# One-hot rows of three token tiles by one comparison, in pooled attention followed by a top-1 mixture of experts

## The chip, the cores and the metric

The kernel runs on one core of a Trainium2 chip. The metric is the device time of one execution in microseconds. The core's engines are TensorE (PE in the profile, its weight loads PEld), VectorE (DVE), ScalarE (ACT), GpSimd (POOL) and SyncE (SP, which issues most DMAs). Each engine takes its instructions in the order in which the program wrote them and waits on semaphores for the others.

## What is computed

Inputs are q, k, v of 8 batches, 8 heads, 576 positions and 64 dimensions, a modality (0 or 1) for each of the 4608 tokens, and the weights of eight experts (512 to 1024 to 512).

```
k_p = k.reshape(B, H, 72, 8, D).mean(axis=3)          # v_p likewise
scores = scale * q @ k_p^T
attn = exp(scores - max) / (sum + 1e-9)
x = (attn @ v_p) as [4608, 512]
logits = x @ w_gate + modality_bias[modality_id]
e_idx = argmax(logits);  gate_w = softmax(logits)[e_idx]
out[token] = gate_w[token] * (relu(x[token] @ w1[e_idx]) @ w2[e_idx])
```

## The kernel before

**Two phases.** The attention comes first. It runs in 20 steps over the batches; a step works on one or two tiles of 128 tokens (36 tiles in all), in two halves of four heads: transposes of q, scores, the maximum (line 533), the subtraction (line 536), the exponential on ScalarE, transposes, and the product with v (lines 590 and 594), which VectorE scales into x and the logits (lines 610 to 616). GpSimd pools k and v of later batches meanwhile by adding halves (`fold`, lines 296 to 298) and multiplies out a remainder of v (line 361, the tile vw). The second phase is the mixture of experts: tokens are sorted by expert into slots of 256, gathered with an indirect DMA, and run through the expert's two matrices (lines 162 and 1143).

**Routing.** Between the phases each token needs a place. This is done in four groups of nine tiles (`route(g)`, lines 646 to 718): the logits are summed over the heads (664), biased (665) and compared with their maximum (666 to 675), gate weights are made (689 to 701), the rank of each token within its expert is a product on TensorE (`pe`, 677 to 688), and the rank is split into a column (`rh`) and a row in the column (`rkm`, then `rkf`, 711 to 715). Lines 716 and 717 make, for each of the nine tiles, the one-hot rows `arow[:, t, :]`: 128 numbers per token in bf16, of which the one at the token's row is 1. `iota_b` holds 0 to 127 in bf16 on every partition; `rkf` has one row number per partition and tile.

**Who uses the rows.** `arow` is the stationary operand of the products that turn ranks into tables of indices: line 776 in `early_table()` (lines 757 to 790), which takes the tiles of the first two groups and is followed by `finish_table` and four gathers (line 142); and line 1039 for the rest, in the second phase.

**What sets the order.** All engines' orders are written by hand. The steps of routing for the groups 0 to 2 aren't written at fixed places: `start(g)` (lines 820 to 826) puts them into a list, `drip`, and `gap(n)` (469 to 473) takes up to n of them off its head where VectorE's program has room: two between a maximum and its subtraction, one behind each of the small steps of `x_dve`, and two at the end of a half step. A step in `held` has TensorE instructions; it stops the list until `release()` writes it at a fixed place once per step of the attention. The list is first in, first out, so every entry that is taken up sooner or later moves all that stand behind it. The last group's steps are written in the second phase (`late`, lines 1091 to 1100): its one-hot rows come as `lr[21:]` in the first slot, with the column numbers behind them.

Of the kernel before, what the change touches and what calls it, by code (L numbers as in the profile page):

```python
# [11 lines left out]
BF16 = mybir.dt.bfloat16  # L12
# [3 lines left out]
ALU = mybir.AluOpType  # L16
# [6 lines left out]
P = 128  # L23
# [7 lines left out]
def kernel(  # L31
# [27 lines left out]
    NSLOT = (NTOK + EARLY_SLOTS * SLOT - 1 - E) // SLOT + E  # L59
    NCOL = 2 * NSLOT  # L60
    GT = 9
    GROUPS = [(GT * i, GT) for i in range(B // 2)]
    T_EARLY = GT * EARLY_GROUPS

# [12 lines left out]
    iota_b = cp.tile([P, P], BF16, name="iota_b")  # L77
# [12 lines left out]
    arow = cp.tile([P, NT, P], BF16, name="arow")  # L90
    oh = cp.tile([P, NT, E], BF16, name="oh")
    cum = cp.tile([P, len(GROUPS) + 1, E], BF16, name="cum")
    gate = cp.tile([P, NT], F32, name="gate")
# [89 lines left out]
    with ExitStack() as actx:  # L183
# [212 lines left out]
        def load_routing():  # L396
# [3 lines left out]
            for z in range(2):  # L400
                mz = mv.rearrange("(i z s) w -> z i s w", z=2, s=S)[z]
                nc.sync.dma_start(mod.rearrange("p (i t) w -> p i (t w)", t=GT)[:, :, 10 * z:10 * z + 8],
                                  mz[:, 0:512, :].rearrange("i (p j) w -> p i (j w)", j=4))
                nc.sync.dma_start(mod.rearrange("p (i t) w -> p i t w", t=GT)[64 * z:64 * z + 64, :, 4, :],
                                  mz[:, 512:S, :].rearrange("i p w -> p i w"))
# [55 lines left out]
        for n, (_, _, ts_) in enumerate(steps):  # L461
            for z, t in enumerate(ts_):
                tile_step[t] = (n, z)
        for g, (t0, n) in enumerate(GROUPS):
            for t in range(t0, t0 + n):
# [130 lines left out]
        def x_dve(t):  # L596
# [5 lines left out]
            if gi == 0:  # L602
                lgs[g] = late_p.tile([P, GT, H, E], F32, tag="lg", bufs=2, name=f"lg_{g}")
            xw = xbs[n if n < NX0 else NX0 + n % (len(xbs) - NX0)]
# [26 lines left out]
        def small(nm, g, shape, dt=F32):  # L631
            if g == len(GROUPS) - 1:
                return cp.tile(shape, dt, name=f"{nm}_{g}")
            return ap.tile(shape, dt, tag=nm, bufs=2, name=f"{nm}_{g}")

        def per_e(a, n):
            return a.rearrange("p (t o) -> p t o", o=1).to_broadcast([P, n, E])

        def per_t(a, n):
            return a.rearrange("p (o e) -> p o e", o=1).to_broadcast([P, n, E])  # L640

        def corner(n):

            return spare[0][:, 1, 4 * SPL + 12 * E:4 * SPL + 12 * E + n]

        def route(g):

            t0, n = GROUPS[g]
            sl = slice(t0, t0 + n)
            lg = small("lgr", g, [P, n, E])  # L650
            ex = small("ex", g, [P, n, E])
            m1 = small("m1", g, [P, n])
            m2 = small("m2", g, [P, n])
            sm = small("sm", g, [P, n])
            dc = small("dc", g, [P, E])
            rs = small("rs", g, [P, n, E])
            rk = small("rk", g, [P, n])
            rki = small("rki", g, [P, n], I32)
            rkm = small("rkm", g, [P, n], I32)
            rkf = small("rkf", g, [P, n])  # L660
            V = nc.vector
            ops = []
            add = ops.append
            add(lambda: V.reduce_sum(lg, lgs[g].rearrange("p t h e -> p t e h"), axis=AX.X))
            add(lambda: V.tensor_add(lg, lg, bias_all[:, sl, :]))
            add(lambda: V.reduce_max(m1, lg, axis=AX.X))

            def sub():
                V.tensor_tensor(lg, lg, per_e(m1, n), op=ALU.subtract)
                nc.scalar.activation(ex, lg, AF.Exp)  # L670
            add(sub)

            add(lambda: V.scalar_tensor_tensor(lg, lg, 0.0, per_t(w8, n), op0=ALU.is_equal, op1=ALU.mult))
            add(lambda: V.reduce_max(m2, lg, axis=AX.X))
            add(lambda: V.tensor_tensor(oh[:, sl, :], per_t(w8, n), per_e(m2, n), op=ALU.is_equal))

            def pe():
                if g == len(GROUPS) - 1:
                    pr = ps_tr.tile([P, n, E], F32, tag="tr", name=f"pr_{g}")
                else:  # L680
                    pr = corner(n * E).rearrange("p (t e) -> p t e", e=E)
                nc.tensor.matmul(pr, tri, oh[:, sl, :], start=True, stop=False)
                nc.tensor.matmul(pr, ones, cum[:, g:g + 1, :].to_broadcast([P, n, E]), start=False, stop=False)
                for i in range(n - 1):
                    m = n - 1 - i
                    nc.tensor.matmul(pr[:, i + 1:n, :], ones, oh[:, t0 + i:t0 + i + 1, :].to_broadcast([P, m, E]),
                                     start=False, stop=(i == n - 2))
                rts[g] = pr
            add(lambda: V.reduce_sum(sm, ex, axis=AX.X))
            add(lambda: V.tensor_scalar_add(sm, sm, 1e-9))  # L690
            add(lambda: V.reduce_sum(dc, oh[:, sl, :].rearrange("p t e -> p e t"), axis=AX.X))

            def gates():
                V.reciprocal(gate[:, sl], sm)
                for z in range(2):
                    b = 2 * g + z
                    nc.sync.dma_start(xs[b * S:b * S + 512, D:D + 1].rearrange("(p j) o -> p (j o)", j=4),
                                      gate[:, t0 + 5 * z:t0 + 5 * z + 4], allow_slow_non_contiguous=True)
                    nc.sync.dma_start(xs[b * S + 512:(b + 1) * S, D:D + 1],
                                      gate[64 * z:64 * z + 64, t0 + 4:t0 + 5], allow_slow_non_contiguous=True)  # L700
            add(gates)
            add(lambda: V.tensor_add(cum[:, g + 1, :], cum[:, g, :], dc))
            held.add(pe)
            add(pe)
            if g >= EARLY_GROUPS:
                add(lambda: V.tensor_tensor(rs, rts[g], per_t(adjv, n), op=ALU.add))  # L706
                add(lambda: V.tensor_mul(rs, rs, oh[:, sl, :]))
            else:
                add(lambda: V.tensor_tensor(rs, rts[g], oh[:, sl, :], op=ALU.mult))
            add(lambda: V.reduce_sum(rk, rs, axis=AX.X))  # L710
            add(lambda: V.tensor_copy(rki, rk))
            add(lambda: V.tensor_single_scalar(rkm, rki, 127, op=ALU.bitwise_and))
            add(lambda: V.tensor_single_scalar(rki, rki, 7, op=ALU.logical_shift_right))
            add(lambda: V.tensor_copy(rkf, rkm))
            add(lambda: V.tensor_copy(rh[:, sl], rki))
            for i in range(n):
                add(lambda i=i: V.tensor_scalar(arow[:, t0 + i, :], iota_b, rkf[:, i:i + 1], None, op0=ALU.is_equal))  # L717
            return ops

        def first_expert():  # L720
# [76 lines left out]
        def at(hook, n, *fns):  # L797
            hook.setdefault(n, []).extend(fns)

        for n, (b, jj, _) in enumerate(steps):  # L800
            if b + 1 < B:
                if jj == 0:
                    m = n if b else n + 1
# [3 lines left out]
                if jj == 1:  # L807
                    m = n if b else n + 1
# [8 lines left out]

        for g in range(len(GROUPS) - 1):
            n = s1_of[2 * g + 1] + 2
            def start(g=g):  # L820
                ops = route(g)
                m = GROUPS[g][1]
                drip.extend(ops[:-m])
                if g == 0:
                    drip.extend(first_expert())
                drip.extend(ops[-m:])
            at(hook_0, n, start)
            if g == EARLY_GROUPS - 1:
                at(hook_0, n, lambda: drip.extend(early_table()))
# [137 lines left out]
        while drip:  # L967
            release()
            gap()
        loads(N + 1)  # L970
        last_route = route(len(GROUPS) - 1)
        for fn in last_route[:7]:
            fn()
# [7 lines left out]
    op = [[ps_op.tile([P, 512], F32, name=f"op{i}_{z}") for z in range(2)] for i in range(2)]  # L981
# [12 lines left out]
    V = nc.vector  # L994
# [106 lines left out]
    t = table(c4 + 6, NCOL, 4)  # L1101
# [189 lines left out]
```

## Time and profile before

| | us |
|---|---|
| three executions | 641.79, 639.85, 642.85 (median 641.79) |
| the profiled execution | 639.47 |
| its span, from the first to the last instruction | 637.8 |
| busy: PE, DVE, ACT, POOL | 601.1, 433.8, 343.8, 198.9 |
| granted TensorE clock, mean over the span | 0.990 |

Busy shares are means over both phases. The attention takes about the first 190 us, and the engines share its work; the mixture of experts takes the rest, and TensorE is busy nearly without a pause in it. For one instruction, its duration says how long it took with its wait for a shared resource, if there was one; how long it holds up its queue is the distance from its start to the start of the next, which can be less, since an instruction of VectorE begins a little before the one ahead has ended.

### The profile page before, as it was taken

How to read it: one execution, taken by the hardware profiler on the slowest of the kernel's cores; microseconds unless marked ns; L12 is line 12 of the kernel's file. 1: busy time of each engine (PE TensorE's matmuls, PEld its weight loads, DVE VectorE, ACT ScalarE, POOL GpSimd, SP SyncE). 2: the span in 40 equal slices, each digit the busy share in tenths (PEclk: the TensorE clock that was granted, in tenths of full speed). 3: DMA queues.
4: the chain of work that ended last, by engine and by line, in shares of the span. 5: the costliest groups of instructions: out<-in, count | busy, mean ns of one | idle time of the engine just before them, and what ended most of it. 6: DMA issues, size and time to landing. Idle time of an engine off the chain costs nothing.

```text
span 637.8 us, 12547 instructions
## 1 busy us (share of the span) xinstructions
PE 601.1 (94%) x4223; PEld 544.8 (85%) x4223; DVE 433.8 (68%) x940; ACT 343.8 (54%) x640; POOL 198.9 (31%) x277
## 2 busy tenths in 40 slices
PE   4799898989899999999999999999999999999992
PEld 3699797888798999999999999999999999999881
DVE  4778989999977578666566566656656566656541
ACT  2667566677441455555555555555556555555530
POOL 6689967563000221320320221231131231131230
PEclk9899999999999999999999999999999999999997
DMA  9999979764201901201210461220225410120120
GB/s 255 290 300 337 350 208 362 223 202 143 67 35 51 315 33 36 68 34 35 68 41 28 148 201 51 67 65 8 63 75 180 145 55 17 52 68 18 51 75 17
DMA packets 63406, 77.18 MB, mean 121 GB/s; under 512 B 15455, under 2 KB 42079, under 8 KB 63328
## 3 DMA queue, kind: packets, MB, share of 16 engines
q1 hardware_dynamic: 57168, 55.98, 28.4%
q0 software_dynamic: 6160, 20.26, 9.7%
q8 instruction: 38, 0.62, 0.4%
q14 instruction: 40, 0.33, 0.2%
HBM read 119.94 MB, written 19.45 MB: 219 GB/s over the span
## 4 chain that ended last, share of the span: by engine, by line
PE 76%; DVE 13%; DMA 7%; issue 1%; ACT 1%; SPq 0%; DVEq 0%; ACTq 0%
PE op L1143 30%; PE hp L162 30%; DMA out_dram<-ob,sidx 6%; PE av L590 3%; PE sc L526 3%; PE xt L153 2%; DVE mx L533 2%; DVE sb L536 2%; PE av L594 2%; DVE xb L614 2%; PE pq L501 1%; PE ph L162 1%; PE pp L555 1%; DVE arow L717 1%; DMA k<-in_k_dram 1%
## 5 line engine op out<-in xcount | busy, mean ns | idle before, releaser
L135 ACT CAST hl<-raw 128x1024 fp32r<-128x1024 f32 x138 | 144.8, 1049 | 138.6 <-PE op L1143 136.6
L162 PE MATMUL hp<-xh,hl 128*128 128x256 f32 x1152 | 186.2, 284 | 0.6 <-issue 0.6
L162 PEld LDWEIGHTS hp<-xh,hl 128*128 128x128 f32 x1152 | 166.0, 189 | 11.5 <-issue 1.0
L138 DVE TENSOR_TENSOR hl<-raw,hl 128x1024 fp32r<-128x1024 f32 x144 | 174.8, 1215 | 0.0
L1143 PE MATMUL op<-hl,hh 128*128 128x512 f32 x554 | 173.5, 394 | 0.0
L1129 POOL DMA_INDIRECT out_dram<-ob,sidx x37 | 51.0, 1379 | 369.3 <-DVE ob L1125 260.2
L166 DVE SCALAR_TENSOR_TENSOR hlo<-hp,hh 128x256 fp32r<-128x256 f32 x139 | 58.8, 423 | 136.6 <-ACT hh L164 136.6
L1143 PE MATMUL op<-hl,hlo 128*128 128x512 f32 x277 | 108.4, 391 | 0.0
L1143 PEld LDWEIGHTS op<-hl,hh 128*128 128x128 f32 x554 | 94.8, 189 | 12.1
L162 PE MATMUL hp<-xl,hl 128*128 128x256 f32 x576 | 92.0, 282 | 0.0
L164 ACT ACTIVATE hh<-hp 128x256 fp32r<-128x256 f32 x139 | 53.4, 384 | 49.6 <-PE hp L162 49.6
L162 PEld LDWEIGHTS hp<-xl,hl 128*128 128x128 f32 x576 | 79.0, 190 | 0.0
L1143 PEld LDWEIGHTS op<-hl,hlo 128*128 128x128 f32 x277 | 52.0, 188 | 11.8
L590 PE MATMUL av<-vw,pt 128*128 128x146 f32 (+1 forms) x320 | 50.9, 299 | 4.9 <-DVE lg L616 3.7
L142 POOL DMA_INDIRECT xg<-xs,gidx x40 | 44.2, 1105 | 17.1 <-issue 8.9
L590 PEld LDWEIGHTS av<-vw,pt 128*128 128x128 f32 (+1 forms) x320 | 40.3, 183 | 7.9 <-DVE lg L616 4.9
L526 PE MATMUL sc<-kt,qt 128*128 128x144 f32 x256 | 38.3, 294 | 1.5 <-DVE rs L706 1.1
L526 PEld LDWEIGHTS sc<-kt,qt 128*128 128x128 f32 x256 | 34.1, 195 | 2.4 <-DVE rs L706 1.3
L156 DVE TENSOR_TENSOR xl<-xt,xh 128x512 fp32r<-128x512 f32 x38 | 24.5, 684 | 15.5 <-ACT xh L155 15.5
L560 ACT COPY pt<-pp 128x512 f32<-128x512 f32 x36 | 21.1, 586 | 25.4 <-PE pp L555 25.0
L533 DVE TENSOR_REDUCE mx<-sc 128x8 f32<-128x576 f32 (+1 forms) x40 | 27.7, 692 | 10.0 <-PE sc L526 7.6
L614 DVE TENSOR_TENSOR xb<-av,r 128x256 f32<-128x256 f32 x72 | 30.4, 422 | 1.6
(226 smaller groups left out, 710.5 us busy)
## 6 DMA issues: line engine op xcount, KB each, us to landing
raw<-in_moe_w_dram SPq DMA_DIRECT2D x304, 256.0 KB
xs<-xb SPq DMA_DIRECT2D x16, 528.0 KB
k<-in_k_dram SPq DMA_DIRECT2D x7, 1024.0 KB
v<-in_v_dram SPq DMA_DIRECT2D x7, 1024.0 KB
q<-in_q_dram SPq DMA_DIRECT2D x6, 1024.0 KB
q<-in_q_dram SPq DMA_DIRECT2D x4, 512.0 KB
v<-in_v_dram SPq DMA_DIRECT2D x16, 128.0 KB
xs<-xb SPq DMA_DIRECT2D x8, 132.0 KB
```

Of the source, the lines that this page charges most:

```text
L135: nc.scalar.copy(hl[f][:, 0, :], raw[f])
L138: eng.tensor_sub(hl[f][:, 1, :], raw[f], hl[f][:, 0, :].bitcast(F32))
L142: nc.gpsimd.indirect_dma_start(out=xgs[(2 * s + tt) % len(xgs)], out_offset=None, in_=xs[0:rows, :], in_offset=IndirectOffsetOnAxis(idx[:, ...
L162: nc.tensor.matmul(ph, hl[f][:, w, d * P:(d + 1) * P], x[:, d, :], start=(n == 0 and d == 0), stop=(n == 2 and d == ND - 1))
L164: nc.scalar.activation(hh, ph, AF.Relu)
L166: nc.vector.scalar_tensor_tensor(hlo, ph, 0.0, hh.bitcast(F32), op0=ALU.max, op1=ALU.subtract)
L526: nc.tensor.matmul(dst, qt[:, i, :], kt[b % NB][:, :, h * SPL:(h + 1) * SPL], start=True, stop=True)
L533: nc.vector.reduce_max(mx, scv, axis=AX.X)
L590: nc.tensor.matmul(av[u][hs, 2 * VC * gg:2 * VC * (gg + 1)], pt[:, c, hs], vw[y][:, c].rearrange("p a x -> p (a x)"), start=(gg == 0), sto ...
L614: nc.vector.tensor_tensor(xo[:, u * D // 2:(u + 1) * D // 2].rearrange("p (h d) -> p h d", h=4), avv[:, :, 0:HD], rb.to_broadcast([P, 4, H ...
L1129: nc.gpsimd.indirect_dma_start(out=out[:, :], out_offset=IndirectOffsetOnAxis(idx.bitcast(U32), 0), in_=ob, in_offset=None, bounds_check=N ...
L1143: nc.tensor.matmul(o[tt], l[:, ts_], hl[f][:, w, D:2 * D], start=(f == 0 and n == 0), stop=(f == NF - 1 and n == 2))
```

## The change

One instruction makes the one-hot rows of three tiles. It compares two tensors of 3 x 128 elements per partition: `iota_b`, repeated for the three tiles, and three columns of `rkf`, each repeated 128 times along the innermost dimension. `rkf` is therefore bf16 now, as `iota_b` is. The nine instructions of a group become three, and `start(g)` cuts three entries off the list's end where it cut nine.

```
+    AW = 3
...
-            rkf = small("rkf", g, [P, n])
+            rkf = small("rkf", g, [P, n], BF16)
...
-            for i in range(n):
-                add(lambda i=i: V.tensor_scalar(arow[:, t0 + i, :], iota_b, rkf[:, i:i + 1], None, op0=ALU.is_equal))
+            for i in range(0, n, AW):
+                add(lambda i=i: V.tensor_tensor(arow[:, t0 + i:t0 + i + AW, :],
+                                                iota_b.rearrange("p (o x) -> p o x", o=1).to_broadcast([P, AW, P]),
+                                                rkf[:, i:i + AW].rearrange("p (t o) -> p t o", o=1).to_broadcast([P, AW, P]),
+                                                op=ALU.is_equal))
...
-                m = GROUPS[g][1]
+                m = GROUPS[g][1] // AW
```

Since the list `drip` is shorter, what stands behind the rows moves too. In the rows below, line numbers of the changed kernel are larger by one up to the one-hot rows and by four behind them; mx and sb are a half step's maximum and subtraction, r to lg the steps of `x_dve`, and the trailing numbers are those of buffers.

VectorE, the second group, at its one-hot rows, before:

```order
L715 CAST rh<-rki_1627 128x9
L717 TENSOR_SCALAR arow<-iota_b,rkf_1629 128x128
L533 TENSOR_REDUCE mx_0_1979<-sc_0_1967 128x8
L717 TENSOR_SCALAR arow<-iota_b,rkf_1629 128x128 x2
L536 TENSOR_TENSOR sb_0_1983<-sc_0_1967,mx_0_1979 128x576
L717 TENSOR_SCALAR arow<-iota_b,rkf_1629 128x128 x2
L533 TENSOR_REDUCE mx_1_2048<-sc_1_2016 128x8
L717 TENSOR_SCALAR arow<-iota_b,rkf_1629 128x128 x2
L536 TENSOR_TENSOR sb_1_2052<-sc_1_2016,mx_1_2048 128x576
L610 TENSOR_SCALAR r_0_2067<-av_0_2040 128x4
L717 TENSOR_SCALAR arow<-iota_b,rkf_1629 128x128
L612 RECIPROCAL r_0_2067<-r_0_2067 128x4
```

The same place now (adjv, sc and s are the first of the early table's steps):

```order
L716 CAST rh<-rki_1621 128x9
L718 TENSOR_TENSOR arow<-iota_b,rkf_1623 128x384
L534 TENSOR_REDUCE mx_0_1973<-sc_0_1961 128x8
L718 TENSOR_TENSOR arow<-iota_b,rkf_1623 128x384 x2
L537 TENSOR_TENSOR sb_0_1977<-sc_0_1961,mx_0_1973 128x576
L534 TENSOR_REDUCE mx_1_2041<-sc_1_2008 128x8
L784 TENSOR_SCALAR adjv<-sc_0_1961 128x8
L785 SCALAR_TENSOR_TENSOR adjv<-adjv,e0oh 128x8
L537 TENSOR_TENSOR sb_1_2045<-sc_1_2008,mx_1_2041 128x576
L611 TENSOR_SCALAR r_0_2060<-av_0_2033 128x4
L786 TENSOR_TENSOR sc_104<-oh,e0oh 128x144
L613 RECIPROCAL r_0_2060<-r_0_2060 128x4
```

The rows end two maxima earlier, and the early table's steps, which stood one step of the attention later, follow them at once.

VectorE, the third group, at its first one-hot rows (h and hl belong to the second phase's first slot), before:

```order
L715 CAST rh<-rki_2265 128x9
L533 TENSOR_REDUCE mx_0_2619<-sc_0_2614 128x8
L717 TENSOR_SCALAR arow<-iota_b,rkf_2267 128x128 x2
L536 TENSOR_TENSOR sb_0_2623<-sc_0_2614,mx_0_2619 128x576
L166 SCALAR_TENSOR_TENSOR h_0_2625<-ph_0_2626,h_0_2625 128x256
L717 TENSOR_SCALAR arow<-iota_b,rkf_2267 128x128 x2
L138 TENSOR_TENSOR hl_2451<-raw_2035,hl_2451 128x1024
```

And now:

```order
L716 CAST rh<-rki_2288 128x9
L534 TENSOR_REDUCE mx_0_2607<-sc_0_2602 128x8
L718 TENSOR_TENSOR arow<-iota_b,rkf_2290 128x384 x2
L537 TENSOR_TENSOR sb_0_2611<-sc_0_2602,mx_0_2607 128x576
L167 SCALAR_TENSOR_TENSOR h_0_2613<-ph_0_2614,h_0_2613 128x256
L718 TENSOR_TENSOR arow<-iota_b,rkf_2290 128x384
L139 TENSOR_TENSOR hl_2445<-raw_2028,hl_2445 128x1024
```

Six tiles' rows stand ahead of sb and h where two tiles' rows stood.

GpSimd, at the last fold of v, the product of line 361 for the last batch and the four early gathers (into xg), before:

```order
L297 TENSOR_TENSOR v_7_1601<-v_7_1601 128x128
L298 TENSOR_TENSOR vp_7_2125<-v_7_1601 128x64
L361 TENSOR_TENSOR vw_140<-vp_7_2125,m_143 128x4x64
L142 DMA xg_80<-xs,gidx_94 128x528
L142 DMA xg_81<-xs,gidx_94 128x528
L142 DMA xg_82<-xs,gidx_94 128x528
L142 DMA xg_83<-xs,gidx_94 128x528
```

And now:

```order
L298 TENSOR_TENSOR v_7_1595<-v_7_1595 128x128
L299 TENSOR_TENSOR vp_7_2124<-v_7_1595 128x64
L143 DMA xg_80<-xs,gidx_94 128x528
L143 DMA xg_81<-xs,gidx_94 128x528
L143 DMA xg_82<-xs,gidx_94 128x528
L143 DMA xg_83<-xs,gidx_94 128x528
L362 TENSOR_TENSOR vw_140<-vp_7_2124,m_143 128x4x64
```

The gathers went ahead of the product. On SyncE the four stores of the third group's gate weights went ahead of one store of x, and on ScalarE its exponential (line 670) ahead of two copies and two exponentials.

## Rows read from the trace of the kernel before

**Rows 1.** The page, shares of the chain that ended last, by line.
```profile
PE op L1143 30%; PE hp L162 30%; DMA out_dram<-ob,sidx 6%; PE av L590 3%; PE sc L526 3%; PE xt L153 2%; DVE mx L533 2%; DVE sb L536 2%; PE av L594 2%; DVE xb L614 2%; PE pq L501 1%; PE ph L162 1%; PE pp L555 1%; DVE arow L717 1%; DMA k<-in_k_dram 1%
```

**Rows 2.** Stretches: length, busy PE PEld DVE ACT POOL (instructions), clock, DMA share, GB/s.
```profile
93.00:101.00 8.00, 7.74 (x61) 7.11 (x60) 7.97 (x26) 4.68 (x13) 6.59 (x10) 1.00 1.05 362
...
126.00:139.00 13.00, 11.28 (x85) 10.19 (x85) 12.71 (x30) 10.03 (x26) 11.68 (x20) 1.00 0.70 226
139.00:148.00 9.00, 9.00 (x90) 8.67 (x89) 8.76 (x37) 8.41 (x21) 0.61 (x1) 1.00 0.38 123
148.00:175.00 27.00, 22.65 (x200) 20.29 (x199) 26.13 (x91) 14.93 (x39) 4.24 (x4) 1.00 0.36 111
175.00:200.00 25.00, 25.00 (x189) 23.45 (x189) 18.36 (x75) 8.14 (x21) 0.00 (x0) 1.00 0.12 45
```

**Rows 3.** The chain in order of time: start us, us, engine, tile, line.
```profile
134.60 1.14 DVE arow L717
...
174.46 0.34 DVE h L166
174.85 0.66 PE pp L555 x4
```

**Rows 4.** Stretches for line 717 alone, one group each: busy DVE, clock, DMA.
```profile
93.00:101.00 8.00, 4.05 (x9) 1.00 1.05 362
126.00:136.00 10.00, 6.74 (x9) 1.00 0.90 289
173.00:180.00 7.00, 1.90 (x9) 1.00 0.16 39
204.00:206.00 2.00, 1.54 (x9) 1.00 0.03 8
```

**Rows 5.** Timeline: start us, us, engine, line, operation, out<-in, sizes, count.
```profile
131.05 2.29 DVE L717 TENSOR_SCALAR arow<-iota_b,rkf 128x128 bf16<-128x128 bf16 x2
...
131.86 1.26 POOL L296 TENSOR_TENSOR v<-v 128x512 f32<-128x512 f32 x1
```

**Rows 6.** Groups of VectorE, whole span: count, busy us, mean ns, idle before.
```profile
L1044 DVE TENSOR_TENSOR bid<-bsel,idw 128x1584 bf16<-128x1584 bf16 x2 | 3.6, 1800 | 0.0
...
L1044 DVE TENSOR_TENSOR bid<-bsel,idw 128x216 bf16<-128x216 bf16 x2 | 0.7, 380 | 0.0
```

**Rows 7.** Groups of VectorE from 60 to 117 us, two operands in SBUF.
```profile
L675 DVE TENSOR_TENSOR oh<-w,m 128x72 bf16<-128x72 f32 x2 | 2.6, 1312 | 0.0
L669 DVE TENSOR_TENSOR lgr<-lgr,m 128x72 f32<-128x72 f32 x2 | 2.5, 1254 | 0.0
L702 DVE TENSOR_TENSOR cum<-cum,dc 128x8 bf16<-128x8 bf16 x2 | 1.3, 646 | 0.0
L665 DVE TENSOR_TENSOR lgr<-lgr,bias_all 128x72 f32<-128x72 f32 x2 | 1.2, 586 | 0.1
L673 DVE SCALAR_TENSOR_TENSOR lgr<-lgr,w 128x72 f32<-128x72 f32 x2 | 0.6, 298 | 0.0
```

**Rows 8.** The same lines from 150 to 200 us, longest and shortest of five.
```profile
L669 DVE TENSOR_TENSOR lgr<-lgr,m 128x72 f32<-128x72 f32 x2 | 0.5, 234 | 0.1
...
L702 DVE TENSOR_TENSOR cum<-cum,dc 128x8 bf16<-128x8 bf16 x2 | 0.3, 130 | 0.0
```

**Rows 9.** Groups of VectorE from 140.8 to 145 us, two of the early table's.
```profile
L784 DVE SCALAR_TENSOR_TENSOR b<-rh,s 128x18 bf16<-128x18 f32 x4 | 0.6, 163 | 0.0
...
L786 DVE TENSOR_TENSOR b<-b,idw 128x72 bf16<-128x72 bf16 x2 | 0.3, 189 | 0.0
```

**Rows 10.** Timeline of GpSimd and VectorE about the early gathers.
```profile
145.64 0.61 POOL L361 TENSOR_TENSOR vw<-vp,m 128x256 f32<-128x256 f32 x1 [6.99 <-PE pk L332]
...
151.03 0.16 DVE L752 TENSOR_SCALAR gidx<-t0ix 128x4 int32<-128x4 f32 x1
...
151.48 1.25 POOL L142 DMA_INDIRECT xg<-xs,gidx  x1 [5.22 <-DVE t0lo L753]
...
155.55 0.19 DVE L387 TENSOR_TENSOR vw<-sc,m 128x32 f32<-128x32 f32 x1 [0.32 <-ACT vw L386]
```

## The prediction

> **What bounds the kernel now.** I read the shares of the chain of waits first, then the engines' busy time by stretch, then the chain in order of time, then the instructions that change. Over the whole span TensorE carries the chain, and the line that changes has about 1% of it [rows 1]. So the change is worth only what it is worth in the stretch where VectorE is late. That is 93 to 175 us: VectorE is busy 7.97 of 8 us, 12.71 of 13 and 26.13 of 27 there, while TensorE has gaps in the same stretches; from 139 to 148 TensorE is full (9.00 of 9) and VectorE nearly so, and from 175 us on TensorE has no gap at all [rows 2]. The chain agrees: it runs over one-hot rows (1.14 us of it from 134.60 us on, a single one) and goes over to TensorE for good at 174.85 us, right behind VectorE's h of 174.46 us [rows 3]. All that can be won or lost lies ahead of that point.
>
> **What a one-hot row costs now.** There are four groups of nine. Nine cost 1.54 us in the last group and 1.90 us in the third, where GpSimd is idle, but 4.05 us in the first and 6.74 us in the second, where GpSimd folds k and v [rows 4]. One free row thus holds its queue for 0.17 us (1.54 over nine). The surplus over 1.90 is waiting: 2.15 us in the first group, 4.84 us in the second, 6.99 over 18 instructions, 0.39 us each. What they wait for is seen in the worst pair: it begins at 131.05 us and ends 2.29 us later, behind two GpSimd instructions that follow each other without a pause, the second at 131.86 for 1.26 us [rows 5].
>
> **What the new instruction costs by itself.** It is a comparison of two tensors over 384 elements. The nearest rows are the products of two bf16 tensors, one of them repeated along its innermost dimension as rkf will be: 380 ns for 216 elements, 1800 ns for 1584 [rows 6]. The slope is 1420/1368 = 1.04 ns per element, so 384 elements take 380 + 168 x 1.04 = 555 ns; less the 0.08 us by which a free row overlaps its successor (about 0.24 long, 0.17 apart) it holds the queue 0.47 us. Three hold it 1.41 us where nine free rows hold it 1.53. **Where nothing waits, nothing is won.** The gain must come from fewer waits: three per group, not nine.
>
> **Does it still wait?** Yes: instructions with two tensors in SBUF wait behind GpSimd too. The five lines of the routing with two such operands took, in the first two groups, 1312, 1254, 646, 586 and 298 ns, two of each [rows 7]; free, they take between 234 and 130 ns [rows 8]. The surplus is about 0.6 us each. The Trainium skill, page "SBUF — State Buffer", section "Who interferes with whom", says the same in general: a VectorE instruction with two SBUF inputs contends with a GpSimd instruction that reads SBUF, and the loser blocks fully; by that rule the new form keeps the old one's fault, and the 1254 ns beside 234 agree. I take w = 0.40 us for one wait, from the one-hot rows, since they stand at the very places; 0.24 (the first group's own, 2.15 over nine) and 0.6 are the ends.
>
> **What moves.** The one-hot rows stand in a queue of small steps that VectorE takes up one or two at a time. With six entries fewer, the steps behind them come sooner. In the second group these are the ten instructions of the early table (from 140.88 us on in the trace). Their durations add up to 1.8 us (two of their six lines stand in [rows 9]), about 1.3 us with the overlaps; eight of them read two SBUF tensors. Today they run where GpSimd is idle (0.61 us busy of 9), afterwards in the stretch in which it is busy 11.68 of 13 us [rows 2]. So in the second group eleven instructions meet the folds, where nine did.
>
> **The sum** (us, against the profiled execution's own 639.47: span 637.8, and 1.7 around it):
> - First group: before 9 x 0.17 + 2.15 = 3.7; after 1.41 + 3 x 0.40 = 2.6. Gain 1.1.
> - Second group: before 1.53 + 4.84 = 6.4; after 1.41 + 1.3 + 11 x 0.40 = 7.1. Loss 0.7. The 1.3 us that leave 140 to 145 us give nothing back there, because that stretch is TensorE's; the other end, if VectorE's lag counts there too, is a gain of 1.3.
> - The five steps after the table (0.16 us for gidx [rows 10], 0.4 to 0.8 together, taken as 0.6) leave the stretch of 148 to 175 us for the one that is TensorE's. Gain 0.6.
> - Third group: two wide instructions before sb and h where two narrow ones stood: 2 x (0.47 - 0.17) = 0.6 lost, right ahead of the hand-over to TensorE at 174.85 us [rows 3]. What follows them lies beside a full TensorE and costs nothing.
> - Fourth group: 1.41 for 1.54 us, beside a full TensorE: nothing.
>
> The sum is 1.1 - 0.7 + 0.6 - 0.6 = 0.4 us gained. In general it is 5.9 - 14 w (w in us): a loss as soon as a wait is over 0.42 us. At 0.24 it is 2.6 gained; at 0.54, the second group's own mean, 1.6 lost; at 0.6, 2.5 lost.
>
> Edits taken at nothing: the cast of rkf to bf16 is the same instruction. GpSimd is held up 0.4 us by each wide instruction that gets in first, at most 2.4 us in all; after the folds it idles (8.4 of 9 us from 139 to 148), and only without that cover would the folds be late. The four gathers go ahead of the last vw product on GpSimd: they took 151.48 to 156.6 us, would start some 9 us sooner, and the product's next neighbour in that tile comes at 155.55 us, so the product may slip from 145.64 to about 148 us unseen [rows 10]; if the gathers waited 8 us for their rows, TensorE's av would. On SyncE four small stores of the gates go ahead of one store of x, whose buffer is not written again for three steps. On ScalarE the third group's exponential comes before two copies and may hold them: 0 to 1 us, taken as 0, since ScalarE is busy 14.93 of 27 us there [rows 2].
>
> **Rivals.**
> 1. *Fewer and shorter waits.* The three instructions of a group fall into pauses of the folds, w is 0.24 as in the first group now, and VectorE's relief from 140 to 145 us counts too: 2.6 + 1.3 = 3.9 us, 637.9. For it: nine rows of the first group already wait only 2.15 us [rows 4]. Against it: the pair stands back to back in front of sb, where the second pays in full.
> 2. *Slower: the early table pays.* Its eight two-operand steps now stand inside the folds of 126 to 139 us and wait like the routing's, 0.6 us each, as do the wide ones: 2.5 us lost, 644.3 against the median; it decides from w = 0.42. For it: [rows 7] are such instructions at just such places. Against it: most of them are tiny (18 elements) and may slip in, as the narrow rows did.
> 3. *Hidden anyway.* Every shift of VectorE is taken up by TensorE, which is busy 11.28 of 13 and 22.65 of 27 us there [rows 2]: no change, 641.8.
> 4. *Not what the price says: two elements per cycle.* The 72-element bf16 products of the early table took 189 ns [rows 9], where the slope above, carried down, gives 380 - 144 x 1.04 = 230, as if for half the elements; if the wide comparison ran at that rate it would take about 0.36 us, hold 0.28, and win 0.19 x 8 = 1.6 us more on the path: 2.0 gained, 639.8. Against it: the rows of [rows 6] are bf16 as well and did not. The Trainium skill, "VectorE: DVE Perf Modes", section "The perf-mode tier table", lists bf16 tensor_tensor from SBUF at twice the base rate, which would be this rival; the 1800 ns for 1584 elements do not show it for an operand repeated innermost.
>
> **How the numbers follow.** Three executions of the kernel before gave 639.85 to 642.85, median 641.79; the profiled one was 2.3 below that. 0.4 off the median is 641.4. A difference of 0.5% (3.2 us) is about what a measurement of this kernel can tell from no change. Chances: the forecast 0.50, rival 1 0.15, rival 2 0.15, rival 3 0.14, rival 4 0.06. The forecast and rivals 3 and 4 lie within 0.5%. Rival 1 at 637.9 is just beyond it and rival 2 at 644.3 just inside, with a spread of 1 to 2 us of the executions on either: faster 0.11, same 0.81, slower 0.08. The range takes in w from 0.24 to 0.6 about the median and some of the executions' own spread: 638.5 to 644.4; under 638.5 the far part of rival 1 is left out, over 644.4 the far part of rival 2, a tenth each.
>
> **What would show it.** In the changed trace: the twelve comparisons near 555 ns in the last two groups (about 360 would be rival 4); in the first two about 2.9 us of busy time for the three (3 x 0.555 + 3 x 0.40); the early table's steps between 130 and 138 us, longer than 0.15 to 0.30 us by 0.4 each; the hand-over to TensorE near 174 to 175 us, and behind it a span of 463 us as before. The prediction is wrong if that hand-over moves by over 3 us, if the part behind it changes, or if TensorE waits for the vw product.

## The result and the profile after

The changed kernel takes **642.94 us** (median of 20, 640.84 to 644.55), the kernel before 640.27 beside it (median of 20): ratio 1.0033, interval 1.0023 to 1.0043, so 2.1 us slower (1.5 to 2.8), where 0.4 us faster was forecast. A second comparison gave 1.0044 (1.0028 to 1.0060). The time lies inside the range (638.5 to 644.4), the direction is not the one forecast; the outcome is nearest to the second rival, though less than half of the loss arose where that rival put it (0.9 of 2.2 us, below).

The comparisons themselves did what the prediction said. The stretches for their line alone (length, busy DVE with its count, clock, DMA share, GB/s):

```profile
93.00:103.00 10.00, 3.03 (x3) 1.00 1.04 367
126.00:136.00 10.00, 2.09 (x3) 1.00 1.02 322
175.00:182.00 7.00, 1.56 (x3) 1.00 0.18 39
207.00:210.00 3.00, 1.48 (x3) 1.00 0.16 48
```

Against [rows 4], 14.23 us of busy time became 8.16; a free one takes about 550 ns, as computed. And yet the stretches of [rows 2] are hardly lighter for VectorE (the same columns; the second phase starts some 3 us later, so the first 3 us of the last row are still attention's):

```profile
93.00:101.00 8.00, 6.53 (x53) 6.21 (x52) 7.86 (x23) 4.70 (x12) 7.53 (x10) 1.00 1.04 365
126.00:139.00 13.00, 11.50 (x92) 10.04 (x89) 12.33 (x38) 10.38 (x26) 10.78 (x17) 1.00 0.81 258
139.00:148.00 9.00, 8.18 (x83) 7.90 (x81) 8.15 (x31) 6.49 (x16) 4.18 (x7) 1.00 0.46 149
148.00:175.00 27.00, 23.96 (x204) 20.68 (x202) 26.31 (x86) 16.52 (x43) 3.23 (x3) 1.00 0.29 93
175.00:200.00 25.00, 23.72 (x180) 22.67 (x180) 18.94 (x62) 8.90 (x23) 0.00 (x0) 1.00 0.16 55
```

The chain in order of time (start us, us, engine, tile, line), beside [rows 3]: the one-hot row that stood in it at 134.60 us is gone, and a step of the early table stands there, nearly twice as long (1.98 us for 1.14); the hand-over to TensorE came at 177.91 us, not 174.85.

```profile
133.37 1.98 DVE adjv L785
...
149.70 2.94 DVE hl L139 x2
...
176.31 0.55 DVE arow L718
...
177.53 0.34 DVE h L167
...
177.91 0.66 PE pp L556 x4
```

**Where the time is**, stage by stage. I take the starts of the same VectorE maximum in both traces. The first pair stands ahead of the first group's rows, the second behind the hand-over (before, after, before, after; timeline, start and duration first):

```profile
93.44 0.75 DVE L533 TENSOR_REDUCE mx<-sc 128x8 f32<-128x576 f32 x1
```
```profile
95.26 0.75 DVE L534 TENSOR_REDUCE mx<-sc 128x8 f32<-128x576 f32 x1
```
```profile
176.52 0.76 DVE L533 TENSOR_REDUCE mx<-sc 128x8 f32<-128x576 f32 x1
```
```profile
179.71 0.74 DVE L534 TENSOR_REDUCE mx<-sc 128x8 f32<-128x576 f32 x1
```

- Ahead of the first: 1.8 us later, in code that is the same. Over all traces of this study that instruction starts between 91.88 and 95.48 us; the second trace of the changed kernel has 92.83. This part is scatter of single executions, and I leave it out of every sum.
- Between the two: 83.08 us before, 84.45 after, **1.4 us lost**; 1.4 in the second trace of the changed kernel too.
- Behind 205 us, where VectorE's routing is over and the two programs are instruction for instruction the same: the op products of hl with hh (op are the products with the experts' second matrix, hp those with the first; hl holds the weights, hh, hlo and xl hold activations) run from 207.7 to 615.9 us before (408.2 us) and from 210.8 to 619.8 after (409.0 us), **0.8 us lost**.

Together 2.2 us, beside 2.1 measured. The prediction has nothing of the second part.

### The profile page after: what moved, and what is told of

Same layout as the page of the kernel before. It is cut to its first block, busy times and chain, and to the rows that moved or that the text cites. A ratio compares the mean times of both kernels' runs of the same rounds, so it can differ in the third digit from the quotient of the medians.

```text
span 641.6 us, 12520 instructions
## 1 busy us (share of the span) xinstructions
PE 604.2 (94%) x4223; PEld 546.3 (85%) x4223; DVE 434.0 (68%) x916; ACT 344.0 (54%) x640; POOL 203.4 (32%) x277
## 4 chain that ended last, share of the span: by engine, by line
PE 73%; DVE 13%; DMA 8%; issue 4%; ACT 1%; SPq 0%; POOL 0%; DVEq 0%; POOLq 0%; ACTq 0%
PE op L1147 28%; PE hp L163 28%; DMA out_dram<-ob,sidx 6%; PE av L591 4%; PE sc L527 3%; PE xt L154 2%; DVE sb L537 2%; PE pp L556 2%; PE av L595 2%; DVE mx L534 2%; PE pq L502 2%; DVE hl L139 1%; PE ph L163 1%; DVE xb L615 1%; DMA k<-in_k_dram 1%
## 5 line engine op out<-in xcount | busy, mean ns | idle before, releaser
L1133 POOL DMA_INDIRECT out_dram<-ob,sidx x37 | 53.4, 1442 | 376.3 <-DVE ob L1129 261.8
## 6 DMA issues: line engine op xcount, KB each, us to landing
v<-in_v_dram SPq DMA_DIRECT2D x16, 128.0 KB
```

The source lines that it names most:

```text
L1133: nc.gpsimd.indirect_dma_start(out=out[:, :], out_offset=IndirectOffsetOnAxis(idx.bitcast(U32), 0), in_=ob, in_offset=None, bounds_check=N ...
```

## The experiments

Theory A: what moved costs. Theory B, its rival: the wide instruction itself costs. Theory C came up on the way: the addresses of tiles cost. In-place kernels put an empty entry where a narrow row stood, so that nothing else moves in `drip`.

**The exchange without the moves.**

```
             for i in range(0, n, AW):
+                add(lambda: None)
                 add(lambda i=i: V.tensor_tensor(arow[:, t0 + i:t0 + i + AW, :],
...
+                add(lambda: None)
...
-                m = GROUPS[g][1] // AW
+                m = GROUPS[g][1]
```

> The exchange alone: three wide comparisons for nine narrow ones, each in the place of the middle one of its three, with empty entries in the places of the other two, so that every other step keeps its place in the queue. Theory A (what costs is what moved: the early table into the folds, the vw product behind the gathers, a pair more ahead of sb): no loss is left, 0 to 1 us below the kernel before. Theory B (what costs is the wide instruction itself, which waits and holds the queue longer where a narrow one slipped in): 1.5 to 2.5 us above the kernel before, as the changed kernel is.

Measured 0.9964 (0.9944 to 0.9984): **2.3 us faster than the kernel before** (1.5 in a second comparison, below). B falls. From 93 to 177 us its trace wins 1.9 us. It wins them at the place of [rows 5] (VectorE and GpSimd, timeline):

```profile
132.43 0.82 DVE L719 TENSOR_TENSOR arow<-iota_b,rkf 128x384 bf16<-128x384 bf16 x1
...
133.37 0.42 DVE L615 TENSOR_TENSOR xb<-av,r 128x256 f32<-128x256 f32 x1
133.39 0.60 POOL L362 TENSOR_TENSOR vw<-vp,m 128x256 f32<-128x256 f32 x1
133.71 0.18 DVE L617 TENSOR_TENSOR lg<-av,r 128x32 f32<-128x32 f32 x1
133.81 0.15 DVE L611 TENSOR_SCALAR r<-av 128x4 f32<-128x4 f32 x1
133.96 1.28 POOL L297 TENSOR_TENSOR v<-v 128x512 f32<-128x512 f32 x1
133.99 0.18 DVE L613 RECIPROCAL r<-r 128x4 f32<-128x4 f32 x1
134.20 0.43 DVE L615 TENSOR_TENSOR xb<-av,r 128x256 f32<-128x256 f32 x1
```

GpSimd's two instructions without a pause, vw and the fold of v, are those of [rows 5] (vw stood at 131.29 us there). What stands beside them now are steps that read PSUM (av) or one small tile, and they run at their free durations. In the kernel before a one-hot row stood there and took 2.13 us. Being small isn't what makes a step free, though: in the changed trace sm, one input of 9 elements, took 1.24 us at 114.61 us, under a fold.

What the first group wins doesn't last. At the maximum at 116.84 us of the kernel before the exchange in place is 0.66 us ahead of it, at that of 127.27 us 0.06. In between TensorE's granted clock shows 0.50, the lower of its two levels (1.2 GHz), where the kernel before has 1.00 (2.4 GHz; the exchange in place first, columns of [rows 2]):

```profile
113.80:117.20 3.40, 3.26 (x18) 2.45 (x17) 3.33 (x16) 1.14 (x4) 3.09 (x7) 0.50 0.21 75
```
```profile
113.80:117.20 3.40, 2.39 (x24) 1.96 (x22) 3.33 (x17) 2.10 (x6) 3.17 (x6) 1.00 0.44 127
```

Ahead of it TensorE had stood idle for 1.3 us from 111.0 us on, in the kernel before for as long from 110.3. All six traces of an exchange in place have such a piece of 3.4 us, from 111.1 to 113.8 us on, and are between 0.5 us ahead and 0.1 behind at 127 us. Of the three traces with the order of the kernel before, one has it (its addresses lowered, below) and loses 0.25 us there. Neither trace of the changed kernel has one between 93 and 177 us.

**The moves without the exchange**: the narrow comparisons, three to an entry.

```
-            for i in range(n):
-                add(lambda i=i: V.tensor_scalar(arow[:, t0 + i, :], ...))
+            for i in range(0, n, AW):
+                add(lambda i=i: [V.tensor_scalar(arow[:, t0 + j, :], iota_b, rkf[:, j:j + 1], None, op0=ALU.is_equal)
+                                 for j in range(i, i + AW)])
```

> The moves alone: the narrow comparisons of the kernel before, three of them to one entry of the queue, so that every step stands where the changed kernel has it. Theory A: 1 to 2.5 us above the kernel before, as the changed kernel is. Theory B: within 0.7 us of the kernel before.

Measured 1.0041 (1.0023 to 1.0059), 2.6 us slower, by 3.0 in its trace from 93 to 177 us. So order alone can cost as much, without the wide form. It doesn't cost it at the same places: 2.3 of the 3.0 us arise ahead of 127 us, where the changed kernel loses nothing. There six narrow rows in a row wait under the folds, TensorE stands idle for 2.1 us from 95.9 us on, and from 98.6 to 102.0 us its clock shows 1.2 GHz. In the second group this kernel loses nothing, in the third 0.8 us. For A in the second group the next run decides.

**Which move.** Six empty entries ahead of the early table (`ops = [lambda: None] * 6 + [count, ...`) put it and all behind it back, and leave the wide rows in three entries in a row:

> The changed kernel with six empty entries ahead of the early table, so that the table, its finish and the gathers stand where the kernel before has them; the wide comparisons of all groups stay as changed. Theory A, with the early table as the main cost: 0 to 0.8 us above the kernel before. Theory B: 1.5 to 2.5 us above it.

Measured 1.0011 (0.9997 to 1.0025), 0.7 us slower; from 93 to 177 us its trace is 0.5 us ahead of the kernel before, 1.9 ahead of the changed one. So of what the changed kernel loses to the exchange in place there (1.4 and 1.9, together 3.3 us), 1.9 is the table and what follows it, and the other 1.3 is that the wide rows stand in a row, two of them ahead of an sb (0.7 us of it in the second group, 0.6 in the third). In the changed kernel the table's step at the place of [rows 5]:

```profile
133.16 0.17 DVE L784 TENSOR_SCALAR adjv<-sc 128x8 f32<-128x8 f32 x1 [0.63 <-ACT pt L575]
133.37 1.98 DVE L785 SCALAR_TENSOR_TENSOR adjv<-adjv,e0oh 128x8 f32<-128x8 f32 x1
133.48 0.61 POOL L362 TENSOR_TENSOR vw<-vp,m 128x256 f32<-128x256 f32 x1
...
134.05 1.27 POOL L297 TENSOR_TENSOR v<-v 128x512 f32<-128x512 f32 x1
```

An instruction over 8 elements, 0.17 us when free, waited for both. Ahead of it VectorE had stood idle for 0.63 us: the table's first step (first line) now comes up before ScalarE's copy of pt has ended, and holds the queue until then.

**The vw product behind the gathers** was an edit taken at nothing. In this kernel the gathers are written behind the product again, by `at(hook_1, s1_of[2 * EARLY_GROUPS + 1] + 2, ...)` in place of the entry in `drip`:

> The changed kernel with the four gathers issued behind the last vw product again, all else as changed. If the vw product that came later met the copy of hl and cost the path what hl grew by (3.03 us for two, 2.35 before), it is 0.7 us below the changed kernel, 1.4 us above the kernel before. If the collision is hidden, as the prediction took it: as the changed kernel, 2.1 us above.

Measured 1.0031 (1.0015 to 1.0048): too wide to tell 0.7 us. The trace tells it: 0.6 us lost from 93 to 177 us instead of 1.4. In the changed kernel the product meets the copies of hl (first fence), here it is over when they begin (second):

```profile
149.62 3.03 DVE L139 TENSOR_TENSOR hl<-raw,hl 128x1024 fp32r<-128x1024 f32 x2
...
150.08 1.48 POOL L362 TENSOR_TENSOR vw<-vp,m 128x256 f32<-128x256 f32 x1
```
```profile
144.87 0.61 POOL L362 TENSOR_TENSOR vw<-vp,m 128x256 f32<-128x256 f32 x1 [7.46 <-PE pk L333]
...
146.19 2.35 DVE L139 TENSOR_TENSOR hl<-raw,hl 128x1024 fp32r<-128x1024 f32 x2
```

**Better places?** If waiting behind the folds is the cost, rows far from them should win more. The first group's rows go ahead of the second group's `pe` (`ops[i:i] = later`), the second group's into the entries of the early table's b steps (`ops[4 + j]` then has two instructions), the third group's two empty entries back.

> The exchange in place, with the first group's three wide comparisons moved back, out of the folds of 93 to 101 us into the second group's steps at about 117 to 126 us, where GpSimd is busy a third of the time. In place they took 1.37, 0.63 and 0.57 us. If waits ahead of 101 us add to the time: 0.9 to 1.6 us below the exchange in place (637.8), so 636.2 to 636.9. If the stretch of 115 to 126 us is TensorE's (10.86 of 11 us busy there) and takes up what VectorE gains ahead of it, as it did with the first group in all kernels so far: as the exchange in place, 637.8.

Measured 0.9988 (0.9970 to 1.0005), 0.8 us faster than the kernel before, no better than in place. They met other folds:

```profile
115.58 1.26 POOL L297 TENSOR_TENSOR k<-k 128x512 f32<-128x512 f32 x1
...
115.79 1.47 DVE L727 TENSOR_TENSOR arow<-iota_b,rkf 128x384 bf16<-128x384 bf16 x1
```

The trace was 2.5 us ahead of the kernel before at 99 us and 0.3 behind at 117; by 127 us every trace with wide rows is within 0.5 us of the kernel before, whatever it had won until then.

> The exchange in place, with the second group's three wide comparisons moved back behind steps of the early table, to 139 to 147 us, where TensorE is full and GpSimd nearly idle. In place they took 0.57, 0.54 and 0.82 us, 1.4 to 1.7 us of VectorE's path from 126 to 139 us. If VectorE sets the pace up to 139 us and TensorE from there on: up to 1.7 us below the exchange in place, so 636.1 to 637.8. If VectorE is the later one from 139 to 148 us as well: no change, or 0 to 0.5 above.

Measured 1.0003 (0.9989 to 1.0017), 2.5 us slower than the exchange in place. The rows don't wait there (0.55 us each), and are paid for nearly in full: up to 140 us the trace runs with that of the exchange in place, at 144 us it has lost 1.2 us to it. TensorE now has gaps from 139 to 148 us, where [rows 2] and the exchange in place show 9.00 of 9:

```profile
139.00:148.00 9.00, 8.69 (x78) 8.14 (x77) 8.34 (x35) 8.28 (x20) 2.02 (x4) 1.00 0.37 121
```

> Both moves, and the third group's comparisons two places back, so that none stands ahead of the sb in front of the hand-over to TensorE at 175 us (one stands there in the exchange in place, 0.55 us). If each place pays for itself: 1 to 3 us below the exchange in place, 634.8 to 636.8. If only the last one does: 0.2 to 0.5 below it.

Measured 0.9992 (0.9978 to 1.0007), 0.5 us faster than the kernel before, slower than in place. In the trace only the third group's move pays: the last step before the hand-over takes 0.34 us less than with a wide row ahead of sb.

> The same places with the narrow comparisons, three to one entry of the queue. Three free narrow ones hold VectorE's queue 0.51 us, a free wide one 0.47. If what counts is the place (a comparison against GpSimd's folds waits, one beside an idle GpSimd doesn't) and the form only where it waits: within 0.7 us of the same places with wide ones. If the wide form is worth something by itself: 1 us or more above.

Measured 1.0001 (0.9982 to 1.0020): 0.6 us above the wide ones at the same places, within the bound. But its trace is 2.3 us behind theirs from 93 to 177 us. Its nine rows at 114 to 118 us also stand in folds; TensorE waits 1.97 us for VectorE there, and from 117.6 to 121.0 us its clock shows 1.2 GHz, which it doesn't with the wide rows. Addresses, which differ, give back 0.8 us of the 2.3 (below); why the times lie closer still isn't shown. Form and place aren't told apart by it.

**Addresses.** In the traces with the bf16 rkf so far the op products behind 205 us took 0.8 to 1.4 us longer, in the two narrow kernels they didn't. rkf of the last group takes 18 bytes per partition instead of 36, and the allocation moves what lies behind it, expert weights and activations among it, 32 bytes down. First rkf gets its old size, in the changed kernel and in the exchange in place:

```
-            rkf = small("rkf", g, [P, n], BF16)
+            rkf = small("rkf", g, [P, 2 * n], BF16)[:, 0:n]
```

> The changed kernel with rkf kept at its old 36 bytes per partition (18 elements of bf16, 9 of them used), so that the tiles allocated behind it stand at their old addresses. With rkf in 18 bytes the last group's shrinks by 32 bytes in the allocation and the expert weights and nearly everything behind them lie 32 bytes lower, at addresses of 32 instead of 0 modulo 64. Theory C (the layout costs): in the kernels with that layout TensorE's op products behind 180 us take 1.0 to 1.7 us more together than in those with the old one; so 1.0 to 1.7 us below the changed kernel, 0.4 to 1.1 us above the kernel before, with the surplus gone from the trace. If that surplus has another cause that goes with the wide instruction: as the changed kernel, 2.1 us above.

Measured 1.0013 (0.9998 to 1.0028), 0.8 us slower instead of 2.1.

> The exchange in place with rkf's old 36 bytes. Theory C: 1.0 to 1.7 us below the exchange in place, so 3.3 to 4.0 us below the kernel before. Otherwise 2.3 us below it.

Measured 0.9964 (0.9950 to 0.9978), as the exchange in place in the first comparison; beside its second one (0.9977, below) 0.8 us less. Its op products take 408.3 us, not 409.3.

> The kernel before with nothing changed but the last group's rkf, allocated 32 bytes larger, so that the tiles behind it lie 32 bytes higher, at 32 instead of 0 modulo 64. Theory C: 1.0 to 1.7 us above the kernel before, with op products slower behind 180 us. Otherwise: no difference.

The kernel before with 32 bytes added to rkf (`[P, n + 8 * (g == len(GROUPS) - 1)]`). Measured 0.9976 (0.9962 to 0.9990), **1.5 us faster**, where 1.0 to 1.7 slower was expected: addresses count, but 32 modulo 64 is not the rule, since both neighbours have it.

> The exchange in place, rkf's old 36 bytes, and the third group's wide comparisons two places back, so that none stands ahead of the sb in front of the hand-over to TensorE. In the trace that move alone took the hand-over 0.34 us ahead. So 0.3 us below the exchange in place with the old layout, 3.6 to 4.3 us below the kernel before.

Measured 0.9966 (0.9951 to 0.9981): 0.3 us can't be told.

Then the kernel before with the weights, and nearly all that lies behind them, at the changed kernel's addresses, and nothing else changed (the last group's rki and rkm in one tile of 72 bytes):

```
-            rki = small("rki", g, [P, n], I32)
-            rkm = small("rkm", g, [P, n], I32)
+            rki2 = small("rki", g, [P, n if g < len(GROUPS) - 1 else 2 * n], I32)
+            rki = rki2[:, 0:n]
+            rkm = small("rkm", g, [P, n], I32) if g < len(GROUPS) - 1 else rki2[:, n:2 * n]
```

> The kernel before with nothing changed but two small integer tiles of the last group in one allocation, which takes 32 bytes less, so that the weights and nearly everything behind them lie where the changed kernel has them, 32 bytes lower. Theory C (these addresses cost 1.2 us of op and hp products behind 180 us): 0.8 to 1.6 us above the kernel before, and the median of the products of hl with hlo at 392 ns, not 389. Otherwise: no difference.

Measured 1.0018 (1.0003 to 1.0032), 1.2 us slower; the median of the products of hl with hlo is 392 ns, 389 before. C, without its rule on 64, holds, with no wide comparison in the program. One line of each trace, the op products of hl with hh (count, ns min/median/max, start of the first and of the last), shows it; before, 32 bytes down, 32 bytes up:

```profile
L1143 PE MATMUL op<-hl,hh x554: 387/395/478, 207.7 to 615.9; 128*128 128x512 f32 x185
```
```profile
L1144 PE MATMUL op<-hl,hh x554: 387/395/478, 207.7 to 616.7; 128*128 128x512 f32 x185
```
```profile
L1143 PE MATMUL op<-hl,hh x554: 387/395/478, 207.9 to 615.7; 128*128 128x512 f32 x185
```

The stretch is 408.2, 409.0 and 407.8 us. Over all twenty traces it is 408.0 to 408.5 at the old addresses (six), 408.9 to 409.6 at the lower (ten), 407.3 to 407.8 at the higher (four): no overlap. Means, over 205 to 616 us, go by nanoseconds: hl with hh 394 before and 396 lower; hp products of xl 282 before, 283 lower, 281 higher.

> The exchange in place once more, with the changed kernel's addresses, on the chip of the next kernel. 0.9964 of the kernel before in the first comparison; by its trace (2.0 us won ahead of 175 us, 1.2 lost behind) 0.7 us below it, so 0.9989.

Measured 0.9977 (0.9962 to 0.9992), 1.5 us faster.

> The exchange in place with everything behind rkf 32 bytes higher than in the kernel before, as in the shifted kernel before, which was 0.7 us shorter behind 180 us in its trace. Theory C: 2.0 us won ahead of 175 us and 0.7 behind, 2.7 us below the kernel before, and 1.9 us below the exchange in place with the lower addresses. If addresses don't move the time: as that.

The edit to the exchange in place is one line:

```
-            rkf = small("rkf", g, [P, n], BF16)
+            rkf = small("rkf", g, [P, 2 * n + 22 * (g == len(GROUPS) - 1)], BF16)[:, 0:n]
```

Measured **0.9925 (0.9907 to 0.9943), 636.19 us, 4.8 us faster than the kernel before**; the fastest of all, and faster than both kernels.

> The changed kernel once more, on the same chip. 2.1 us above the kernel before; in the trace 1.4 us lost from 93 to 175 us, 1.2 behind 180 us, and what stands ahead of 93 us, where the code is the same, tells how far that stretch scatters by itself.

Measured 1.0044 (1.0028 to 1.0060); 1.4 us lost from 93 to 177 us, 0.7 behind, as in the first trace, and 0.6 us gained ahead of 93.

> The changed kernel, nothing moved, with everything behind rkf 32 bytes higher than in the kernel before. By the traces: 1.4 us lost from 93 to 175 us, 0.7 to 1.0 won behind 180 us, so 0.4 to 0.7 us above the kernel before (640.8 to 641.1). If the higher addresses are worth some 2 us more than the trace shows: 1 to 2 us below it.

Measured 0.9985 (0.9971 to 0.9998), 1.0 us faster than the kernel before: with other addresses the changed kernel no longer loses.

> The exchange in place, the third group's wide comparisons two places back, and the higher addresses. By the traces: 2.2 to 2.5 us won ahead of 175 us and 0.7 to 1.0 behind 180 us, 2.9 to 3.5 us below the kernel before, about 637.2. If the 4.8 us of the exchange in place with the higher addresses are real: 635.3.

Measured 0.9933 (0.9912 to 0.9954), 636.27 us, as the exchange in place with the same addresses.

**What stays open.** Places and addresses added up from the traces meet the measured time within its interval for the kernels at the old addresses (the late narrow one misses it by 0.1 us) and for eight of the ten at the lower ones. The four at the higher addresses came out 1.0 to 2.2 us faster than their sums, and the two runs of the exchange in place at the lower ones 1.0 and 1.5. Whether the rest lies in the scatter ahead of 93 us, one trace each can't tell. Nor is it known which tile's address counts, or by which rule.

## Why the prediction was wrong

**What bounds the kernel**: half right. All that its order changed was won or lost between 93 and 177 us, and TensorE takes over for good behind h. But "from 139 to 148 TensorE is full" was read as "VectorE's time costs nothing there". The second group's rows put there were paid for with 1.2 of 1.4 us. Both engines were nearly full (8.76 of 9 for VectorE in [rows 2]); a full TensorE doesn't say that the other has slack. Nor does all that VectorE wins from 93 us on reach the hand-over. Counted from the maximum at 95.26 us, the changed kernel was 0.56 us ahead of the kernel before at 118.09 us and 0.10 at 128.99; TensorE is busy 10.80 of 10.80 us from 117.2 to 128.0 in it. In the exchange in place the loss goes with the piece at 1.2 GHz.

**Price and waits**: right, the waits on average only. 555 ns forecast, 550 measured; two elements per cycle (rival 4) is out. Three comparisons of the first group took 3.03 us and of the second 2.09 (2.9 forecast for each): w was 0.46 and 0.15 us. The early table's ten steps in the folds, before `product`, took 4.9 us where they took 2.0 (the prediction has 1.8): 2.9 us of waits, 0.36 each, where eight waits of 0.40 are 3.2. With these waits, 0.34 us on average, the prediction's own 5.9 - 14 w gives 1.2 us won, so the size of the waits isn't what failed. An instruction over 8 elements waited 1.8 of its 1.98 us. The rule of the Trainium skill, page "SBUF — State Buffer", section "Who interferes with whom", that a VectorE instruction with two SBUF inputs and a GpSimd one that reads SBUF block each other, agrees, and is told there without regard to size. That the tiny steps "may slip in", my objection to rival 2, was wrong where GpSimd leaves no pause.

**The sum**, by stretches between the same maxima, the changed kernel against the kernel before:

| | forecast | trace |
|---|---|---|
| first group (33.83 us before, 33.73 after) | 1.1 won | 0.1 won |
| second group, to 143.88 us (16.61, 17.49) | 0.7 lost | 0.9 lost |
| finish steps, to 172.73 us (28.85, 28.71) | 0.6 won | 0.1 won |
| third group (3.79, 4.53) | 0.6 lost | 0.7 lost |
| behind 205 us | nothing | 0.8 lost |

- *First group*, the first step that failed. The pair ahead of sb held the queue 2.30 us (from 95.92 to 98.22), not 1.74, because the first stood under the fold of 95.61 us and the second under that of 96.96, which follows without a pause; the two narrow rows there had held it 1.09. And the exchange of the seven narrow rows behind it gave back 1.30 us, not 1.75: several stood between r, its reciprocal and xb, each of which needs the one ahead. From r to xb it was 0.50 us with two free rows in between (from 97.50 us) and is 0.40 without (from 100.27): such a row cost 0.05 us, not the 0.17 of a row among rows.

```profile
95.61 1.27 POOL L297 TENSOR_TENSOR v<-v 128x512 f32<-128x512 f32 x1
95.92 2.37 DVE L718 TENSOR_TENSOR arow<-iota_b,rkf 128x384 bf16<-128x384 bf16 x2
96.96 0.92 POOL L298 TENSOR_TENSOR v<-v 128x256 f32<-128x256 f32 x1
97.96 0.65 POOL L299 TENSOR_TENSOR vp<-v 128x128 f32<-128x128 f32 x1
98.22 0.74 DVE L537 TENSOR_TENSOR sb<-sc,mx 128x576 f32<-128x576 f32 x1
```

- *Second group*: right in sign and size, by luck. From the maximum at 127.27 us to the one at 143.88 the rows held VectorE's queue 1.5 us instead of 5.6, the table's steps 4.3 instead of 1.1: 0.9 us won, where 0.7 lost was forecast. The loss came from two things that the prediction has at nothing there: the finish steps, which now stand in this stretch (0.6 us), and 1.1 us more in which VectorE stands idle, above all ahead of the table's first step (0.63) and the finish's first (0.26), which come up before a copy of ScalarE's has ended.
- *Third group*: right in sign and size.
- *Finish steps*: 0.6 was there, and the vw product took it back. "The product may slip unseen" looked only at the next user of its tile ([rows 10]); what it met was VectorE's copies of hl, the same contention as everywhere else in this case. With the gathers behind it again this stretch wins 0.8 us.
- *Behind 205 us*, the step that failed outright: the edit of rkf was taken at nothing. "The cast of rkf to bf16 is the same instruction" is true, but the tile's size changed, and with it the address of nearly everything behind it: 0.8 us, 1.2 by the times of the kernel before with only that. Nothing in the profile page shows an address; "a span of 463 us as before" was taken for granted.

Of the rivals, the second was the mechanism for the early table, but not at its price: 0.36 us a wait, not 0.6. In the fourth, 0.19 x 8 is 1.5 and not 1.6. What would have shown the prediction wrong, a hand-over moved by over 3 us, did come (3.06), of which 1.8 was scatter ahead of 93 us; the part behind it changed too.

## What to carry to other kernels

A cheaper form can be worth what it saves only if the instructions around it keep their places: here the exchange won 2.3 us (1.5 in the second comparison), and letting the queue close up behind it turned that into a loss of 2.1, because other two-operand steps slid under GpSimd's unbroken stretches, and steps came to the head of the queue before their inputs were there. After an edit that shortens a shared queue, look at who now stands beside each such stretch, and when a tile changes size, keep its bytes, or compare stretches of the program that the edit doesn't touch: a constant drift there meant here that addresses had moved. Read the granted clock of each stretch before comparing it: a piece at 1.2 GHz cost 0.25 us in one trace of the same order.

## What the runs showed beside that

- The same VectorE step, behind 93 us of identical code, starts at 91.88 us in one trace and 95.48 in another:

```profile
91.88 0.75 DVE L534 TENSOR_REDUCE mx<-sc 128x8 f32<-128x576 f32 x1
```
```profile
95.48 0.75 DVE L534 TENSOR_REDUCE mx<-sc 128x8 f32<-128x576 f32 x1
```

  The shifts arise in the first 57 us in some traces and from 57 to 80 us in others. Thirteen traces win 1.6 to 1.7 us on the kernel before between 19.6 and 24.1 us, the other six at most 0.4; these six and the kernel before are the ones in which TensorE's clock shows 1.2 GHz for a piece that begins at 24.8 to 26.3 us. The delay is there before the clock falls; what makes it isn't shown. Behind 93 us the two traces of the changed kernel agree within 0.02 us up to 177 us, the two of the exchange in place within 0.13. So a single pair of traces can be compared here stage by stage, between the same two instructions, and not by absolute times.
- 32 bytes of address and nothing else made the kernel before 1.2 us slower downwards and 1.5 us faster upwards.
